# Gram of eight units per call, in four array tiles and two PSUM banks

## The chip, the cores and the metric

The kernel runs on one core of a Trainium2 chip. The core has four compute engines with queues of their own: TensorE (PE, with its weight loads shown apart as PEld), VectorE (DVE), ScalarE (ACT) and GpSimd (POOL); SyncE (SP) issues the DMAs. The metric is device time in microseconds, lower is better. The kernel before takes 352.01 us (median of three runs, 351.21 to 354.52).

## The reference

A gated delta-rule attention (batch 4, 8 heads, 768 tokens, head size 48) feeds a gated convolution with two 384 x 384 projections. All is float32.

```python
for t in range(S):
    kt, vt, bt = (k_n[:, :, t], v[:, :, t], beta[:, :, t, None])
    y[:, :, t] = np.einsum('bhd,bhde->bhe', q[:, :, t], state)
    v_old = np.einsum('bhde,bhd->bhe', state, kt)
    state = state + bt[:, :, :, None] * np.einsum('bhd,bhe->bhde', kt, vt - v_old)
...
for k in range(K):
    gate_pre += conv_w[k][None, None, :] * xp[:, k:k + S, :]
gate = 1.0 / (1.0 + np.exp(-gate_pre))
val = x @ w_val
return (gate * val @ w_out).astype(np.float32)
```

`k_n` is `k` divided by its norm (plus 1e-6); `x` is `y` with the heads side by side, 384 wide; `xp` is `x` with four zero tokens ahead.

## The kernel before

**Chunks and groups.** The 768 tokens are cut into 12 chunks of 64, and two chunks make a group, so there are six groups (`g` 0 to 5). In a chunk each of the 32 (batch, head) pairs has its own small problem. The pairs come two by two: a *unit* is one such double, with one pair in the upper and one in the lower partitions, 16 units a chunk (`NP`) and 32 a group (`NU`). Inside a chunk the recurrence is solved in closed form: it needs the products of all keys of the chunk with each other and with the queries (the Gram), the inverse of a triangular matrix made of them, and the state at the chunk's start.

**Preparing a group (`prep`).** SP loads keys and queries feature by feature into one of three `KQ` buffers, eight units at a time, so four loads make a group. `gram(c, h)` then multiplies K by [K, Q] for four units (`QB`) into one PSUM bank of 128 x 512: one pair's 48 features stand in partitions 64 to 111 and go to PSUM partitions 0 to 63, the other's in 0 to 47 and go to 64 to 127. Each is a matmul of 48 rows, 64 columns of weights and 128 streamed columns, in its own quarter of the array (array tile). Two of the four quarters are used. A call is eight matmuls, which the trace shows as 16 instructions, since each float32 matmul is run in two passes. ACT copies each bank to SBUF (`gevac`, tile `GL`). `diag` (ACT) collects the diagonal blocks in `D1`, and DVE turns them with a large transpose (`trans_in`, `TLP<-D`). Then follows a long chain on DVE, with some large products on POOL: 18 small steps for the norms and coefficients (`coef`), rows and merges that build the inverse, and two transposes out (`trans_out`, tiles `TTR` and `TNA`). With `TTR` PE forms the off-diagonal blocks in two levels (`lev1`, tile `z`; `lev2`, tile `t`).

**The chain of chunks (`chain`).** For each chunk PE multiplies with the state (`e`), DVE adds that to V (`eevac`), PE applies the inverse (`u`) and updates the state (`SPS`), ACT copies both out, PE forms the output `y`, ACT copies it, and SP moves parts of it with six small DMAs (`X<-YS`) to the tile `X`. Some of these matmuls are issued in turns: `eumul` interleaves the 16 matmuls of `e` for one half with the 16 of `u` for the other. `e` uses the same two array tiles as `gram`, `u` the other two, and they write different PSUM banks.

**The gated convolution (`moe`).** For each chunk and each of three feature blocks: two taps of the convolution on PE (`conv`), three on DVE (`tap`), a sigmoid on ACT (`sig`), the projection `val` on PE, and the product on DVE (`gate`). Then two `out` calls on PE, copied by ACT and stored.

**What sets the order.** Every step is entered in a plan (`add`) with its engine and what it reads and writes. `ORDER`, a table of step numbers found beforehand, is the order in which the steps are issued; each engine runs its own in that order. A negative number -n in it stands for n filler matmuls on zeros (`keep_warm`, `SPS<-ZW`), which keep TensorE's clock up and whose result nobody reads. PSUM banks come from two pools of three: pool "w" serves `gram`, `z`, `t`, `val` and `out`, pool "c" the rest of the chain and `conv`. A bank is taken by the step with `take` and given back by the one with `give`; a step that takes waits until a bank has been given back.

The host lays K and Q out for the KQ load: for each chunk an array of 112 rows, the first of a double's features in rows 64 to 111, the second's in 0 to 47, for all 16 units.

Of the kernel before, what the change touches and what calls it, by code (L numbers as in the profile page):

```python
# [16 lines left out]
B, H, S, D = 4, 8, 768, 48  # L17
C = 64
# [74 lines left out]
]  # L93


# [729 lines left out]
```

## Time and profile before

| what | value |
|---|---|
| median of three runs | 352.01 us |
| time of the profiled execution | 352.4 us |
| span of its instructions | 350.7 us |
| granted TensorE clock, mean | 0.946 |

The profile shows this one execution. "Busy" is time in which an engine runs instructions; in a row of a group it is followed by the mean of one instruction, then by the idle time just before such instructions and by what ended that. In a row of the timeline the first number is the start and the second the length in microseconds, a final x32 the number of instructions merged in the row, and a bracket the idle time before it. A row by stage gives the window, its length, then the busy time and instruction count of each engine, the granted clock, the DMA share and GB/s. How the groups follow each other is read from the first `z` matmul of each, the step for which PE needs DVE's `TTR`: 64.4, 108.6, 155.2, 203.9, 246.0 and 298.8 us for groups 0 to 5; PE's last `out` ends at 346.1. Rows of the profile that carry the argument stand in the prediction.

### The profile page before, as it was taken

What the parts mean: (1) busy time and instruction counts of PE and PEld (TensorE: products, weight loads), DVE (VectorE), ACT (ScalarE), POOL (GpSimd) and SP (SyncE); (2) the same over time, 40 slices, a digit from 0 to 9 for tenths busy, and PEclk for the clock granted to TensorE, in tenths of its full rate; (3) what the DMA queues carried; (4) which work ended last, traced back from release to release, by engine and by line L of the source; (5) the groups of instructions that cost most, each with busy time, mean ns of one, the idle gap of its engine ahead of it and who ended that gap; (6) DMA issues with size and microseconds to landing.
All of it is one profiled execution on the core that took longest, in us unless ns stands there. A gap on an engine that the chain in (4) does not pass through costs nothing.

```text
span 350.7 us, 13815 instructions
## 1 busy us (share of the span) xinstructions
PE 318.4 (91%) x5998; PEld 262.1 (75%) x5998; DVE 260.8 (74%) x565; ACT 194.3 (55%) x428; POOL 123.0 (35%) x92
## 2 busy tenths in 40 slices
PE   8769997689299799999799999999988999999994
PEld 5768997689288687878668778777677787687872
DVE  5038999999789876999956999789885689612550
ACT  6643400898149853379764797447973421974221
POOL 6425047034891026512068400545204564000000
PEclk9985899668769999999999999999999999999999
DMA  7999711036274534144574435135253332101122
GB/s 201 249 269 277 190 52 47 7 104 187 67 170 133 151 110 118 32 141 126 140 200 119 136 99 152 50 85 158 56 152 104 80 78 49 38 15 36 36 45 45
DMA packets 20283, 39.47 MB, mean 113 GB/s; under 512 B 8112, under 2 KB 11312, under 8 KB 20224
## 3 DMA queue, kind: packets, MB, share of 16 engines
q1 hardware_dynamic: 20224, 38.60, 41.5%
q8 instruction: 47, 0.77, 0.9%
q14 instruction: 12, 0.10, 0.1%
HBM read 32.69 MB, written 4.72 MB: 107 GB/s over the span
## 4 chain that ended last, share of the span: by engine, by line
PE 62%; DVE 21%; ACT 6%; DMA 5%; issue 3%; POOL 1%; SPq 0%; ACTq 0%; DVEq 0%
PE val L704 14%; PE out L715 12%; PE conv L689 9%; PE gram L351 6%; DMA KQ<-in_kq_dram 5%; PE e L570 5%; PE u L570 3%; PE SPS L570 3%; PE y L638 3%; PE y L640 2%; DVE PR L426 2%; DVE TT__83 L433 2%; PE z L450 2%; PE t L470 2%; ACT D L214 2%
## 5 line engine op out<-in xcount | busy, mean ns | idle before, releaser
L694 DVE SCALAR_TENSOR_TENSOR conv<-X,CW,conv 128x256 f32<-128x256 f32 x108 | 48.5, 486 | 19.7 <-PE conv L689 12.8
L351 PE MATMUL gram<-KQ 48*64 48x128 f32 x768 | 54.0, 295 | 6.1 <-DMA KQ<-in_kq_dram 5.6
L704 PE MATMUL val<-X,WV 128*128 128x256 f32 x216 | 53.4, 388 | 1.3 <-ACT GL L214 1.3
L351 PEld LDWEIGHTS gram<-KQ 48*64 48x64 f32 x768 | 47.7, 147 | 8.5 <-issue 3.5
L715 PE MATMUL out<-WO,GT 128*128 128x384 f32 x144 | 50.3, 490 | 0.0
L704 PEld LDWEIGHTS val<-X,WV 128*128 128x128 f32 x216 | 39.5, 189 | 8.5 <-ACT GL L214 1.4
L214 ACT ACTIVATE GL<-gram 128x512 f32<-128x512 f32 x48 | 28.1, 596 | 23.1 <-PE gram L351 22.7
L689 PE MATMUL conv<-X,DW 128*128 128x256 f32 x144 | 37.9, 399 | 0.5 <-DMA X<-YS 0.5
L715 PEld LDWEIGHTS out<-WO,GT 128*128 128x128 f32 x144 | 26.8, 189 | 15.0 <-issue 0.2
L570 PE MATMUL u<-VT,BD 64*64 64x48 f32 x768 | 31.1, 230 | 7.2 <-DVE VT L622 6.2
L570 PEld LDWEIGHTS u<-VT,BD 64*64 64x64 f32 x768 | 27.3, 144 | 10.7 <-issue 8.7
L548 POOL TENSOR_SCALAR_AFFINE_SELECT AQ<-GL 64x1024 f32<-64x1024 f32 x24 | 28.3, 1180 | 16.5 <-PE y L638 12.2
L214 ACT ACTIVATE D<-GL 32x512 f32<-32x512 f32 (+1 forms) x36 | 22.7, 631 | 19.7 <-DVE TT__83 L433 19.1
L758 PEld LDWEIGHTS SPS<-ZW 128*128 128x128 f32 x242 | 31.3, 210 | 2.8 <-issue 2.7
L758 PE MATMUL SPS<-ZW 128*128 128x128 f32 x242 | 32.9, 298 | 0.0
L708 DVE TENSOR_TENSOR GT<-val,GT 128x256 f32<-128x256 f32 x36 | 15.0, 420 | 20.8 <-PE val L704 18.8
L689 PEld LDWEIGHTS conv<-X,DW 128*128 128x128 f32 x144 | 26.2, 193 | 5.1 <-issue 0.6
L342 POOL TENSOR_TENSOR VT<-VT,NRM 128x768 f32<-128x768 f32 x12 | 17.7, 1477 | 35.1 <-DMA VT<-in_vt_dram 27.7
L638 PE MATMUL y<-AQ,US 112*64 112x64 f32 x384 | 29.1, 233 | 0.0
L638 PEld LDWEIGHTS y<-AQ,US 112*64 112x64 f32 x384 | 25.9, 146 | 3.6 <-issue 2.2
L698 ACT ACTIVATE GT<-conv 128x256 f32<-128x256 f32 x36 | 13.4, 387 | 27.1 <-DVE conv L694 27.0
L640 PE MATMUL y<-AQ,US 128*48 128x64 f32 x384 | 28.0, 230 | 0.0
(97 smaller groups left out, 591.2 us busy)
## 6 DMA issues: line engine op xcount, KB each, us to landing
KQ<-in_kq_dram SPq DMA_DIRECT2D x24, 448.0 KB, 4.7
KF<-in_kf_dram SPq DMA_DIRECT2D x11, 448.0 KB, 3.9
VT<-in_vt_dram SPq DMA_DIRECT2D x12, 384.0 KB, 4.1
AQ<-in_qf_dram SPq DMA_DIRECT2D x24, 192.0 KB, 3.6
KT<-in_kt_dram SPq DMA_DIRECT2D x12, 384.0 KB, 3.5
out_dram<-OS SPq DMA_DIRECT2D x48, 96.0 KB, 2.2
AQ<-in_w_val_dram SPq DMA_DIRECT2D x3, 384.0 KB, 11.0
AQ<-in_w_out_dram SPq DMA_DIRECT2D x3, 384.0 KB, 12.7
```

The source lines that it names most:

```text
L214: A.activation(out=out, in_=in_, func=AF.Copy, **kw)
L342: G.tensor_tensor(out=VT[c], in0=VT[c], in1=NRM[:, c * NP:(c + 1) * NP].unsqueeze(2).to_broadcast([128, NP, D]), op=ALU.mult)
L351: PE.matmul(p[64 * a:64 * a + 64, 128 * j:128 * (j + 1)], x[:, 0:C], x, start=True, stop=True)
L548: G.affine_select(out=AQ[c][r0:r0 + 64, j], in_=GL[r0:r0 + 64, c * NP:(c + 1) * NP, 64:128], pattern=[[0, NP], [1, C]], compare_op=ALU.is_ ...
L570: return lambda: PE.matmul(*a, stop=True, **k)
L638: PE.matmul(p[0:64, C * j:C * j + C], US[ch % 3][0:112, 0, h, D * j:D * j + 64], AQ[c][0:112, 0, pp, :], start=True, stop=True)
L640: PE.matmul(p[64:112, C * j:C * j + C], us[:, 1, h, j, :], AQ[c][:, 1, pp, :], start=True, stop=True)
L689: PE.matmul(p[:, 0:B * C].rearrange("p (b t) -> p b t", t=C), DW[:, m, i, :], x[:, m, :, k:k + C], start=(i == 0), stop=(i == len(PTAPS) - 1))
L694: V.scalar_tensor_tensor(out=p, in0=x[:, m, :, k:k + C], scalar=CW[:, m, k:k + 1], in1=p, op0=ALU.mult, op1=ALU.add)
L704: PE.matmul(p[:, 0:B * C].rearrange("p (b t) -> p b t", t=C), WV[:, k, 128 * m:128 * m + 128], xs[:, k], start=(k == 0), stop=(k == NKT - 1))
L715: PE.matmul(bank["o", ch, i][:, 0:DM], GT[k][:, 2 * i:2 * i + 2, :].rearrange("p b t -> p (b t)"), WO[:, k, :], start=(k == 0), stop=(k == ...
L758: PE.matmul(SPS[0][:, 384:512], ZW, ZW, start=False, stop=True, skip_group_check=True)
```

## The change

A call of `gram` now takes eight units. It holds two banks and runs four matmuls for each step `j`: two units, one in the first four of the load (`s` = 0) and one in the second four (`s` = 1), each with both its pairs. For the second four units the host swaps the rows: the pair that goes to PSUM partitions 0 to 63 has its features in rows 0 to 47, and the other in 64 to 111. So the four matmuls of a step fall into all four quarters of the array; the two that share PSUM partitions come from different rows and write different banks. There are four calls a group instead of eight, each with two `gevac` copies. The first of the two banks is taken by a step of its own, `gram_bank`, without an instruction.

```diff
+        def gram_bank(c, h):
+            bank["g", g, c, 2 * h] = wps("gram")
+
         def gram(c, h):
-            p = bank["g", g, c, h] = wps("gram")
-            kq_ = KQ[(4 * g + 2 * c + h // 2) % 3]
+            bank["g", g, c, 2 * h + 1] = wps("gram")
+            kq_ = KQ[(4 * g + 2 * c + h) % 3]
             for j in range(QB):
-                for a, r in ((0, slice(64, 112)), (1, slice(0, D))):
-                    x = kq_[r, QB * (h % 2) + j, :]
-                    PE.matmul(p[64 * a:64 * a + 64, 128 * j:128 * (j + 1)], x[:, 0:C], x, start=True, stop=True)
+                for a in range(2):
+                    for s in range(2):
+                        r = 64 * (a ^ s ^ 1)
+                        x = kq_[r:r + D, QB * s + j, :]
+                        PE.matmul(bank["g", g, c, 2 * h + s][64 * a:64 * a + 64, 128 * j:128 * (j + 1)], x[:, 0:C], x,
+                                  start=True, stop=True)
...
-        for i in range(8):
-            c, h, n = i // 4, i % 4, 4 * g + i // 2
-            if h % 2 == 0:
-                add("SP", 1.0, load, (KQ[n % 3], kq[2 * g + c, h // 2]), w=[("KQ", n % 3)], kind="LK")
-            add("PE", 0.87, gram, (c, h), cols=1536, r=[("KQ", n % 3)], w=[("gp", g, i)], take="w")
-            add("ACT", 0.5, gevac, (c, h), r=[("gp", g, i)], w=[("GL", gb, i), ("GQ", gb, i)], give="w")
+        for i in range(4):
+            c, h, n = i // 2, i % 2, 4 * g + i
+            tk = [("KQ", n % 3)]
+            add("SP", 1.0, load, (KQ[n % 3], kq[2 * g + c, h]), w=tk, kind="LK")
+            add("PE", 0, gram_bank, (c, h), r=tk, w=["gb"], take="w")
+            add("PE", 1.0, gram, (c, h), cols=3072, r=tk + ["gb"], w=[("gp", g, i)], take="w")
+            for s in range(2):
+                add("ACT", 0.5, gevac, (c, 2 * h + s), r=[("gp", g, i)], give="w",
+                    w=[("GL", gb, 2 * i + s), ("GQ", gb, 2 * i + s)])
...
-    kq = kq.reshape(nch, 112, 2, HB, 2 * C).transpose(0, 2, 1, 3, 4)
+    kq = kq.reshape(nch, 112, 2, HB, 2 * C).transpose(0, 2, 1, 3, 4).copy()
+    kq[:, :, 0:D, QB:], kq[:, :, 64:112, QB:] = kq[:, :, 64:112, QB:].copy(), kq[:, :, 0:D, QB:].copy()
```

The table `ORDER` is new throughout; two of its lines:

```diff
-    1, 4, 8, 2, 16, 110, 5, 160, 3, 65, 162, 6, 70, 9, 10, 7, 11, 12, 13, 161, 0, 14, 75, 15, 17, 24, 64, 18, 19,
+    -1, 8, 16, 65, 160, 9, 70, -1, 3, 1, 2, 7, 75, -1, 10, 11, 12, -1, 13, -2, 14, 17, 0, 4, 6, -1, 15, 24, 64, 18,
```

It holds 147 filler matmuls where the old one held 121; 25 of the new ones stand behind group 1's first `z`, where the old table has none. What it moves is shown at three places. Names are those of the program: a tile's name, its number, then its size.

The first place is SP's queue at the start, before: the DMAs in the order of issue. `KQ0`, `KQ1`, `KQ2` are the three Gram buffers (the fourth load of group 0 is the second one to `KQ0`), `VT` is V, `KF` is K for the chain, `AQ0<-in_qf` is Q, the weights come through `AQ1`.

```order
L219 DMA AQ1_79<-in_w_val_dram 128x768
L219 DMA VT1_75<-in_vt_dram 128x768
L219 DMA KQ0_67<-in_kq_dram 112x1024
L219 DMA AQ0_78<-in_qf_dram 48x1024
L219 DMA KQ1_68<-in_kq_dram 112x1024
L219 DMA BE_108<-in_beta_dram 128x192
L219 DMA AQ0_78<-in_qf_dram 48x1024
L219 DMA KQ2_69<-in_kq_dram 112x1024
L219 DMA AQ1_79<-in_w_val_dram 128x768
L219 DMA KF1_77<-in_kf_dram 112x1024
L219 DMA VT0_74<-in_vt_dram 128x768
L219 DMA KQ0_67<-in_kq_dram 112x1024
```

The same queue now, up to the third block of `w_val`:

```order
L221 DMA AQ1_79<-in_w_val_dram 128x768
L221 DMA KQ0_67<-in_kq_dram 112x1024
L221 DMA KQ1_68<-in_kq_dram 112x1024
L221 DMA BE_108<-in_beta_dram 128x192
L221 DMA KQ2_69<-in_kq_dram 112x1024
L221 DMA AQ1_79<-in_w_val_dram 128x768
L221 DMA KQ0_67<-in_kq_dram 112x1024
L221 DMA KT0_70<-in_kt_dram 128x768
L221 DMA AQ1_79<-in_w_val_dram 128x768
```

Both VT loads, both Q loads and the KF load have gone behind the fourth KQ load.

The second place is PE around the first `z` of group 1, before. `X_98` and `X_99` belong to chunks 0 and 1, `GL_81` to group 1, and the `gram` rows to group 3.

```order
L570 MATMUL e<-US_95,KF_76 64x48 x16
L689 MATMUL conv<-X_98,DW 128x256 x2
L570 MATMUL SPS_121<-US_94,KT_71 48x48 x16
L689 MATMUL conv<-X_98,DW 128x256 x2
L758 MATMUL SPS_120<-ZW 128x128 x6
L450 MATMUL z<-TTR,GL_81 32x32 x16
L351 MATMUL gram<-KQ_67 64x128 x16
L450 MATMUL z<-TTR,GL_81 32x32 x16
L351 MATMUL gram<-KQ_68 64x128 x16
```

The same place now:

```order
L700 MATMUL conv<-X_98,DW 128x256 x6
L581 MATMUL SPS_121<-US_94,KT_71 48x48 x16
L715 MATMUL val<-X_98,WV 128x256 x6
L700 MATMUL conv<-X_99,DW 128x256 x2
L715 MATMUL val<-X_98,WV 128x256 x3
L700 MATMUL conv<-X_99,DW 128x256 x4
L769 MATMUL SPS_120<-ZW 128x128
L726 MATMUL out<-WO,GT_101 128x384 x6
L769 MATMUL SPS_120<-ZW 128x128
L458 MATMUL z<-TTR,GL_81 32x32 x32
L358 MATMUL gram<-KQ_67 64x128 x16
L769 MATMUL SPS_120<-ZW 128x128 x3
```

All of chunk 0's `conv`, `val` and `out` and chunk 1's `conv` now stand ahead of this `z` (three `conv` of two matmuls each, three `val` of three, two `out` of three more than before), and fillers stand behind it.

The third place is DVE ahead of group 1's transpose `TTR`, before. The `conv` rows are the taps, `GT` rows the gates, `VT<-e` is `eevac`.

```order
L433 TENSOR_REDUCE TT__83<-PR_85 128x16x4
L426 TENSOR_TENSOR PR<-ZT,TT__83 128x512
L694 SCALAR_TENSOR_TENSOR conv<-X_98,CW,conv 128x256
L433 TENSOR_REDUCE TT__83<-PR 128x16x4
L694 SCALAR_TENSOR_TENSOR conv<-X_98,CW,conv 128x256
L433 TENSOR_REDUCE TT__83<-D_86 128x16x4
L622 TENSOR_TENSOR VT_74<-e,VT_74 128x384
L440 STREAM_TRANSPOSE TNA<-TT__83 128x32x32
L438 STREAM_TRANSPOSE TTR<-TT__83 128x32x32
```

The same place now:

```order
L705 SCALAR_TENSOR_TENSOR conv<-X_98,CW,conv 128x256 x8
L434 TENSOR_TENSOR PR<-ZT,TT__83 128x512
L719 TENSOR_TENSOR GT_101<-val,GT_101 128x256
L441 TENSOR_REDUCE TT__83<-PR 128x16x4
L705 SCALAR_TENSOR_TENSOR conv<-X_98,CW,conv 128x256
L441 TENSOR_REDUCE TT__83<-D_86 128x16x4
L719 TENSOR_TENSOR GT_101<-val,GT_101 128x256
L448 STREAM_TRANSPOSE TNA<-TT__83 128x32x32
L705 SCALAR_TENSOR_TENSOR conv<-X_99,CW,conv 128x256 x2
L719 TENSOR_TENSOR GT_101<-val,GT_101 128x256
L446 STREAM_TRANSPOSE TTR<-TT__83 128x32x32
```

Eleven taps instead of two and three gates instead of none stand ahead of `TTR`; the taps of `X_99` need chunk 1's output.

122 rows, old and new, of the table ORDER are left out of this document.

## The prediction

> **What bounds the kernel now.** I read the page's busy shares and slices first, then the chain that ended last, then busy time by stage, and last the timeline of single calls.
>
> ```profile
> span 350.7 us, 13815 instructions
> PE 318.4 (91%) x5998; PEld 262.1 (75%) x5998; DVE 260.8 (74%) x565; ACT 194.3 (55%) x428; POOL 123.0 (35%) x92
> ...
> PE   8769997689299799999799999999988999999994
> ...
> DVE  5038999999789876999956999789885689612550
> ...
> PEclk9985899668769999999999999999999999999999
> ```
>
> PE is busy 91% of the span, but not for one reason throughout. In the first third DVE shows the nines; from slice 13 on it is PE, at full clock. I cut the span at the first level-1 matmul (`z`) of group 0 and of group 1, at those of groups 4, 5 and at the end of PE's work.
>
> ```profile
> core 0: us, PE busy (x) PEld busy (x) DVE busy (x) ACT busy (x) POOL busy (x), PEclk, DMA share, GB/s
> 0.00:64.38 64.38, 52.84 (x486) 47.46 (x487) 44.46 (x93) 24.40 (x45) 26.70 (x25) 0.89 0.67 175
> 64.38:108.63 44.25, 36.81 (x892) 33.37 (x892) 39.52 (x73) 30.24 (x64) 25.09 (x17) 0.73 0.41 112
> 108.63:346.20 237.57, 228.73 (x4620) 181.25 (x4620) 176.79 (x401) 139.17 (x321) 71.23 (x50) 1.00 0.36 96
> ...
> 203.90:246.00 42.10, 41.97 (x944) 33.81 (x940) 36.60 (x88) 26.96 (x61) 14.61 (x9) 1.00 0.41 112
> ...
> 298.80:346.20 47.40, 46.76 (x797) 35.58 (x796) 18.23 (x40) 22.84 (x57) 0.22 (x1) 1.00 0.14 31
> ```
>
> So there are three parts. Up to 108.63 the loads and then DVE's preparation of groups 0 and 1 decide; much of PE's work there is filler on zeros. From 108.63 on PE is busy 228.73 of 237.57 us, with 8.8 idle. The last 47.4 us are nearly pure PE.
>
> **The cheaper Gram.** A call before is eight logical matmuls, in two array tiles.
>
> ```profile
> L351 PE MATMUL gram<-KQ 48*64 48x128 f32 x768 | 54.0, 295 | 6.1 <-DMA KQ<-in_kq_dram 5.6
> ...
> 109.02 1.96 PE L351 MATMUL gram<-KQ 48*64 48x128 f32 x32
> 110.91 0.45 PE L450 MATMUL z<-TTR,GL 32*32 32x32 f32 x32
> ...
> 123.22 0.22 PE L570 MATMUL e<-US,KF 48*64 48x48 f32 x2
> 123.23 0.23 PE L570 MATMUL u<-VT,BD 64*64 64x48 f32 x2
> 123.28 0.23 PE L570 MATMUL e<-US,KF 48*64 48x48 f32 x2
> 123.29 0.23 PE L570 MATMUL u<-VT,BD 64*64 64x48 f32 x2
> ...
> 130.83 1.10 PE L570 MATMUL e<-US,KF 48*64 48x48 f32 x32
> ```
>
> Two calls (32 instructions, two passes for each logical matmul) hold PE from 109.02 to 110.91, so 0.945 us each, or 118 ns for each round of two tiles. Do four tiles fit in a round? The kernel already has that pattern: `e` and `u` together start four matmuls (two `e`, two `u`, in four array tiles and two banks) every 0.06 us, while `e` alone needs 1.10 us for 32 instructions, 0.069 for two. Four cost no more than two. The Gram streams 128 columns where these stream 48, so the nearest row is its own round; I take 0.945 us for the new call of eight units. The other end is 1.89, no overlap. With 24 new calls for 48 old, PE loses 24 x 0.945 = 22.7 us of work. Of this only the calls of groups 3 to 5 lie behind 108.63: 12 x 0.945 = 11.3 us on the path. The other half lies in stretches where PE waits or fills, and I cost it at nothing.
>
> One thing speaks against this price: two of the four tiles share the same rows of the array. If a tile's weight load could not hide behind the other tile's matmul, each of the eight rounds would add about an `e`/`u` round, and a call would take 0.945 + 8 x 0.06 = 1.43 us; the saving on the path would be 12 x (1.89 - 1.43) = 5.5 us instead of 11.3. `e` and `u` share rows in the same way and still start a round every 0.06 us, so I leave it to the rivals. By the Trainium skill (TensorE: Matmul & The Clock Gate, Part 3, "What overlaps and what doesn't") a weight load overlaps running matmuls only if its row group differs, which is that case; the `e` and `u` rows don't agree with it, though at 48 columns only.
>
> **Work moved ahead of group 1's `z`.** Three `conv`, three `val` and two `out` calls of chunks 0 and 1 now stand before group 1's first `z`, and nine more taps and three more gates before DVE's transpose TTR of group 1.
>
> ```profile
> L694 DVE SCALAR_TENSOR_TENSOR conv<-X,CW,conv 128x256 f32<-128x256 f32 x108 | 48.5, 486 | 19.7 <-PE conv L689 12.8
> L704 PE MATMUL val<-X,WV 128*128 128x256 f32 x216 | 53.4, 388 | 1.3 <-ACT GL L214 1.3
> L715 PE MATMUL out<-WO,GT 128*128 128x384 f32 x144 | 50.3, 490 | 0.0
> L689 PE MATMUL conv<-X,DW 128*128 128x256 f32 x144 | 37.9, 399 | 0.5 <-DMA X<-YS 0.5
> L708 DVE TENSOR_TENSOR GT<-val,GT 128x256 f32<-128x256 f32 x36 | 15.0, 420 | 20.8 <-PE val L704 18.8
> ...
> 42.98 16.57 PE L758 MATMUL SPS<-ZW 128*128 128x128 f32 x146
> ```
>
> Calls are 36 `conv` of 37.9/36 = 1.05 us, 36 `val` of 1.48, 24 `out` of 2.10. So 3 x 1.05 + 3 x 1.48 + 2 x 2.10 = 11.8 us of PE work leaves the PE-bound part for a part in which PE fills. What hides it there is DVE's preparation; if that cover were short, at most the 11.8 us would come back. On SP a VT load now stands among the six X<-YS transfers of chunk 0 and waits for chunk 1's `u`; chunk 0's `conv` stands behind that `u` on PE anyway, so I cost it at nothing, and at one load's landing (4.1 us, below) if it is late. DVE pays 9 x 48.5/108 + 3 x 0.417 = 5.3 us ahead of TTR. In its stage DVE idles 44.25 - 39.52 = 4.7 us, some of it behind POOL products that these taps can cover. The price is between 0.6 and 5.3; I take 3.
>
> Against that the new order puts 25 filler matmuls behind group 1's `z` (none before): 73 of them took 16.57 us, so 25 x 0.227 = 5.7 us, if none stands in a wait. They have no reader. PE work behind `z` of group 1: 228.73 - 11.3 - 11.8 + 5.7 = 211.3 us.
>
> **The start.** These are the chain's first links, and the loads that stand ahead of the fourth KQ load.
>
> ```profile
> 2.20 6.75 DMA KQ<-in_kq_dram
> 8.99 1.99 PE gram L351 x32
> 10.99 10.72 DMA KQ<-in_kq_dram
> 21.85 1.10 PE gram L351 x16
> 23.47 0.54 ACT AQ L271
> 24.01 0.59 ACT GL L214
> ...
> 26.58 2.09 DVE TLP L364
> ...
> KQ<-in_kq_dram SPq DMA_DIRECT2D x24, 448.0 KB, 4.7
> KF<-in_kf_dram SPq DMA_DIRECT2D x11, 448.0 KB, 3.9
> VT<-in_vt_dram SPq DMA_DIRECT2D x12, 384.0 KB, 4.1
> AQ<-in_qf_dram SPq DMA_DIRECT2D x24, 192.0 KB, 3.6
> AQ<-in_w_val_dram SPq DMA_DIRECT2D x3, 384.0 KB, 11.0
> ...
> 32.58 2.91 POOL L342 TENSOR_TENSOR VT<-VT,NRM 128x768 f32<-128x768 f32 x2 [3.28 <-DVE QUOT L334]
> ```
>
> The fourth KQ load took 10.72 us because 3.8 MB had been issued ahead of it; with its own 0.45 MB, 4.26 MB had landed by 21.85 us, 0.195 MB per us. Two VT, two qf and the KF load now come behind it: 2 x 384 + 2 x 192 + 448 KB = 1.6 MB, so it could land 8 us sooner. But ACT evacuates this Gram only after it has converted the third `w_val` block, whose load now has about 3.4 MB up to its end: 3.4/0.195 = 17.5 us. From 23.47, where ACT began that block, to DVE's transpose at 26.58 are 3.1 us; with 0.5 for the landing and a second evacuation the transpose starts near 21.5. I take 5 us of gain; the ends are 0 (a load put back is missed) and 8. DVE's order from there to TTR of group 0 is nearly the old one, so the gain carries through.
>
> **The sum**, on the profiled execution, 350.7 us of span and 352.4 of time (352.01 is the median of the runs, 0.4 lower). First `z` of group 1: 108.6 - 5 + 3 = 106.6. From there to the first `z` of group 5, PE was busy 228.7 - 46.8 = 182.0 of 190.2 us, idle 8.2; its work is now 182.0 - 11.3 - 11.8 + 5.7 - 1 = 163.6 (1 us more falls in the tail, one `out` for one `conv`), and with the old idle time 172. DVE has a say here: it was busy 176.8 - 18.2 = 158.6, now 153.3, and in the stage where it had least slack, 203.90 to 246.00, it still idled 5.5 us. Four such stages make 153.3 + 22 = 175.3. The two engines bound this part at nearly the same length, so waits of one on the other add; I take 177 where 190.2 stood. Tail 48.4, then 4.5 us from the last matmul to the end. Span 106.6 + 177 + 48.4 + 4.5 = 336.5; time 336.5 + 1.7 = 338.2, less 0.4: **338 us**, 4% faster.
>
> **The rivals.**
>
> - *The start does not come earlier, or DVE eats it.* Against it: of the loads put back, VT was first read at 32.58, by a POOL step that waited for DVE. For it: DVE's 5.3 us may count in full. The time is 338 + 5 without the start, 338 + 7.3 with both: 343 to 345.
> - *Four tiles do not run side by side.* No row shows 128 columns in four tiles. With unhidden weight loads 12 x 0.48 = 5.8 us come back, 344; with nothing overlapping 11.3, 349. The `e` and `u` rows speak against both.
> - *DVE alone becomes the bound, and PE's saving stays unused.* Were the four stages to keep their length, 190.2 instead of 177, the time would be 351. Against it: DVE's longest idle rows there are waits for PE, 18.8 us for `val`, 12.8 for `conv`.
> - *Slower: two banks at once.* `gram`, `z`, `t`, `val` and `out` share three banks, and a Gram call now holds two until ACT, in its own order, has copied both; `val` and `out` then follow each other on the third.
>
> ```profile
> L214 ACT ACTIVATE GL<-gram 128x512 f32<-128x512 f32 x48 | 28.1, 596 | 23.1 <-PE gram L351 22.7
> ...
> 121.52 1.56 PE L704 MATMUL val<-X,WV 128*128 128x256 f32 x6 [1.33 <-ACT GL L214]
> ```
>
>   Even now a `val` waited 1.33 us for such a copy. If each of the 12 late Gram calls and of the 33 `val` calls behind `z` paid a wait of half that, 45 x 0.67 = 30 us would go against the 14 gained: 368. It decides once about 21 of the 45 calls wait so long. For it: two copies of 0.596 us take longer than a call of 0.945, so Gram calls back to back are bound by ACT. Against it: the order spreads the calls between `z`, `e` and `u`, which need other banks or only one. The Trainium skill (TensorEngine Tiling (Array Packing), "PSUM Bottleneck") has the general form: tiling speeds up TensorE but not the evacuation of PSUM, which may then be the bound.
>
> **How the numbers follow.** The likeliest, 332 to 342, has 0.52. The start or DVE rival has 0.18, four tiles 0.07, DVE alone 0.10, banks 0.08 (as far as they make it slower than before). An even better end, all of the start's 8 us and the fillers in waits (338 - 3 - 5.7 = 329), has 0.05. The 80% range is 329 to 348. About 1%, 3.5 us, is what a measurement of this kernel can tell from no change: faster than that 0.81, within it 0.11, slower 0.08.
>
> **What would show it.** Gram rows of the new kernel: four starts each round and about 0.95 us for 32 instructions (right), or 1.4 to 1.9 (wrong). DVE's first large transpose near 21.5 us instead of 26.58; the first `z` of group 1 near 106.6. PE's idle rows behind it: waits for ACT's Gram copies of more than 10 us in all would mean banks, waits for TTR or for gates of more than 15 us would mean DVE. PE's busy time should fall to about 300 us. I am wrong if the start is still at 26 us or if `val` waits for ACT.

## The result, and the profile after

The changed kernel takes 337.19 us (median of 4 runs, 335.16 to 340.48), beside 351.61 us for the kernel before on the same chip (4 runs, 349.62 to 354.52). The ratio is 0.956 with a 95% interval of 0.946 to 0.967: 4.4% faster. The forecast was 338.0 us. Three further measurements of the same kernel, below, gave 334.9 to 335.6 us. Some executions are in a slower state, which the ratios leave out (of e6 two of six are left, so its 352.80 us and its ratio below don't match), and no stage length is read from the profiles of e1, e4, e6 and e11, which were taken in it.

The page of the changed kernel, its span, busy times and slices:

```profile
span 336.5 us, 13878 instructions
...
PE 308.9 (92%) x6050; PEld 251.0 (75%) x6050; DVE 261.8 (78%) x565; ACT 193.3 (57%) x428; POOL 124.7 (37%) x92
...
PE   8936999699779979999999999999999999999994
...
DVE  5368999999698994999997899896998779511640
...
PEclk9987599755997998999999999999999999999999
```

PE is busy 308.9 us where it was 318.4 (the forecast said about 300), DVE has the same work as before. The slices tell the same story as before: DVE's nines in the first third, PE's nines from there on.

Cut at the first `z` of group 0 and of group 1 (first three rows, columns as in the prediction's rows by stage), and one stage of the PE-bound part, groups 3 to 4:

```profile
0.00:58.50 58.50, 48.15 (x499) 42.57 (x499) 44.51 (x93) 23.35 (x45) 26.07 (x25) 0.85 0.71 186
58.50:109.95 51.45, 44.12 (x924) 37.94 (x924) 45.61 (x87) 34.83 (x72) 25.09 (x18) 0.77 0.32 88
109.95:336.50 226.55, 216.67 (x4629) 170.52 (x4628) 171.68 (x388) 135.10 (x313) 73.50 (x49) 0.99 0.41 106
...
191.57:241.41 49.84, 49.30 (x1022) 39.18 (x1018) 43.12 (x99) 32.83 (x75) 21.67 (x16) 1.00 0.41 109
```

The first part is 5.9 us shorter, the second 7.2 longer, the third 15.5 shorter (226.55 us, where before 350.7 - 108.63 = 242.1 stood). By the first `z` of each group, with two of the later measurements of the same kernel beside it:

| stretch, us | before | forecast | after | e0 | e8 |
|---|---|---|---|---|---|
| start to `z` of group 0 | 64.4 | 59.4 | 58.5 | 58.3 | 57.3 |
| `z` of group 0 to group 1 | 44.3 | 47.2 | 51.5 | 49.4 | 49.7 |
| `z` of group 1 to group 5 | 190.2 | 177 | 173.8 | 172.5 | 172.3 |
| `z` of group 5 to the end | 51.9 | 52.9 | 52.8 | 52.9 | 53.0 |
| span | 350.7 | 336.5 | 336.5 | 333.1 | 332.3 |

The groups that answer to those shown of before, and the fillers:

```profile
L705 DVE SCALAR_TENSOR_TENSOR conv<-X,CW,conv 128x256 f32<-128x256 f32 x108 | 49.9, 484 | 14.2 <-PE conv L700 12.1
L715 PE MATMUL val<-X,WV 128*128 128x256 f32 x216 | 52.5, 390 | 0.0
...
L358 PE MATMUL gram<-KQ 48*64 48x128 f32 x768 | 33.4, 311 | 10.2 <-DMA KQ<-in_kq_dram 8.5
...
L769 PE MATMUL SPS<-ZW 128*128 128x128 f32 x294 | 43.7, 302 | 0.4 <-ACT US L643 0.4
```

The same 768 `gram` instructions now fill 33.4 us of PE instead of 54.0, though the mean of one is no shorter (311 ns, before 295): they overlap. `val` no longer waits at all. The fillers fill 43.7 us in 294 instructions, two for each filler; before it was 32.9 us in 242. One call in the timeline:

```profile
156.17 0.94 PE L769 MATMUL SPS<-ZW 128*128 128x128 f32 x6
157.03 1.10 PE L358 MATMUL gram<-KQ 48*64 48x128 f32 x32
158.07 1.13 PE L700 MATMUL conv<-X,DW 128*128 128x256 f32 x4
```

Eight units, 32 instructions, hold PE from 157.03 to 158.07, 1.04 us. The forecast had 0.945; before, 32 instructions took 1.89. The row above it shows three fillers (six instructions) in 0.86 us, 0.287 each where the forecast had 0.227.

The start, in the chain of work that ended last:

```profile
8.67 1.08 PE gram L358 x32
9.77 0.88 ACT GL L216 x2
10.65 7.23 DMA AQ<-in_w_val_dram
17.98 0.55 ACT AQ L273
18.53 0.98 ACT GL L216 x2
...
21.49 2.06 DVE TLP L372
```

The fourth KQ load has left the chain. The third block of `w_val` stands in it instead, and DVE's first large transpose starts at 21.49 instead of 26.58.

What PE waited for between the first `z` of group 1 and that of group 5:

```profile
PE y L649 <- issue: 1.9, 1, 1.9
PE y L649 <- DMA AQ<-in_qf_dram: 0.7, 1, 0.7
PE SPS L769 <- ACT US L643: 0.4, 2, 0.2
PE SPS L581 <- issue: 0.4, 1, 0.4
PE gram L358 <- ACT GL L216: 0.2, 1, 0.2
```

Here the columns are the sum in microseconds, the number of waits and the longest. For a Gram copy PE waited 0.2 us in all. "issue" is a wait for nothing that the profile shows; the last section has more on it.

### The profile page after: what moved, and what is told of

Read it like the earlier page. It is cut to its first block, busy times and chain, and to the rows that moved or that the text cites. A ratio compares the mean times of both kernels' runs of the same rounds, so it can differ in the third digit from the quotient of the medians.

```text
span 336.5 us, 13878 instructions
## 1 busy us (share of the span) xinstructions
PE 308.9 (92%) x6050; PEld 251.0 (75%) x6050; DVE 261.8 (78%) x565; ACT 193.3 (57%) x428; POOL 124.7 (37%) x92
## 4 chain that ended last, share of the span: by engine, by line
PE 60%; DVE 14%; ACT 8%; DMA 7%; POOL 4%; issue 3%; SPq 3%; POOLq 0%; ACTq 0%; DVEq 0%
PE out L726 14%; PE val L715 11%; PE conv L700 7%; PE gram L358 4%; PE e L581 4%; PE u L581 3%; PE SPS L769 3%; PE y L649 3%; SPq L221 3%; PE SPS L581 2%; PE y L651 2%; PE z L458 2%; DMA AQ<-in_w_val_dram 2%; PE t L478 2%; DMA X<-YS 2%
## 5 line engine op out<-in xcount | busy, mean ns | idle before, releaser
L705 DVE SCALAR_TENSOR_TENSOR conv<-X,CW,conv 128x256 f32<-128x256 f32 x108 | 49.9, 484 | 14.2 <-PE conv L700 12.1
L421 POOL TENSOR_TENSOR PR<-TLP,TT__83 128x768 f32<-128x768 f32 x5 | 10.6, 2118 | 97.0 <-DVE TT__83 L416 97.0
L769 PE MATMUL SPS<-ZW 128*128 128x128 f32 x294 | 43.7, 302 | 0.4 <-ACT US L643 0.4
L769 PEld LDWEIGHTS SPS<-ZW 128*128 128x128 f32 x294 | 39.4, 210 | 5.1 <-issue 3.6
L358 PE MATMUL gram<-KQ 48*64 48x128 f32 x768 | 33.4, 311 | 10.2 <-DMA KQ<-in_kq_dram 8.5
L216 ACT ACTIVATE GL<-gram 128x512 f32<-128x512 f32 x48 | 27.1, 596 | 16.7 <-PE gram L358 16.2
L358 PEld LDWEIGHTS gram<-KQ 48*64 48x64 f32 x768 | 26.1, 156 | 13.6 <-issue 9.3
L649 PE MATMUL y<-AQ,US 112*64 112x64 f32 x384 | 31.0, 237 | 4.7 <-issue 4.0
L651 PE MATMUL y<-AQ,US 128*48 128x64 f32 x384 | 29.1, 233 | 0.0
L633 DVE TENSOR_TENSOR VT<-e,VT 128x384 f32<-128x384 f32 x22 | 12.3, 557 | 20.1 <-PE e L581 14.1
L637 ACT ACTIVATE US<-u 64x384 f32<-64x384 f32 x24 | 11.6, 483 | 27.9 <-PE u L581 27.8
```

Source lines behind the costliest of these rows:

```text
L216: A.activation(out=out, in_=in_, func=AF.Copy, **kw)
L358: PE.matmul(bank["g", g, c, 2 * h + s][64 * a:64 * a + 64, 128 * j:128 * (j + 1)], x[:, 0:C], x, start=True, stop=True)
L633: V.tensor_tensor(out=v, in0=bank["e", ch, h][:, 0:HB * D].rearrange("p (u x) -> p u x", x=D), in1=v, op=ALU.add)
L649: PE.matmul(p[0:64, C * j:C * j + C], US[ch % 3][0:112, 0, h, D * j:D * j + 64], AQ[c][0:112, 0, pp, :], start=True, stop=True)
L651: PE.matmul(p[64:112, C * j:C * j + C], us[:, 1, h, j, :], AQ[c][:, 1, pp, :], start=True, stop=True)
L705: V.scalar_tensor_tensor(out=p, in0=x[:, m, :, k:k + C], scalar=CW[:, m, k:k + 1], in1=p, op0=ALU.mult, op1=ALU.add)
```

## The experiments

All were timed in five rounds against the kernel before. They ran in three groups (e0 to e3, e4 to e7, e8 to e11); the kernels of a group shared a chip and its runs of the kernel before, so each is compared with the unedited kernel of its own group (e0, e4, e8). Those three differ by up to 0.007 among themselves, so smaller differences than about 1% are not read.

| run | edit | us | ratio to before, 95% |
|---|---|---|---|
| e0 | none | 334.90 | 0.944 [0.939, 0.949] |
| e1 | Gram in two array tiles | 349.16 | 0.981 [0.975, 0.987] |
| e2 | five loads back ahead of the fourth KQ load | 343.09 | 0.966 [0.960, 0.972] |
| e3 | without 25 fillers | 339.36 | 0.957 [0.952, 0.962] |
| e4 | none | 335.60 | 0.949 [0.943, 0.956] |
| e5 | new Gram call, old order | 379.84 | 1.077 [1.071, 1.083] |
| e6 | moved work put back | 352.80 | 0.988 [0.978, 0.998] |
| e7 | halo copy first on POOL | 337.90 | 0.954 [0.947, 0.961] |
| e8 | none | 335.07 | 0.950 [0.945, 0.956] |
| e9 | e5 with 104 fillers more | 381.38 | 1.083 [1.078, 1.088] |
| e10 | e6 with 40 fillers more | 349.67 | 0.994 [0.990, 0.998] |
| e11 | 22 fillers more in group 0's stage | 342.54 | 0.970 [0.963, 0.976] |

**The yardsticks.**

> The changed kernel itself, unedited, as the yardstick for the three kernels run beside it. Both theories: 335 to 339 us, a ratio of 0.956 to the kernel before.

> The changed kernel unedited once more, as the yardstick for the three beside it: a ratio of 0.944 to 0.957 to the kernel before.

> The changed kernel once more, unedited, as the yardstick of the three runs beside it: 0.944 to 0.949 of the kernel before, as in its two earlier runs.

The unedited kernel came out at 0.944, 0.949 and 0.950. Together with the first measurement (0.956) this is one kernel at 335 to 337 us.

**e1: is it the four array tiles?** The call keeps eight units and two banks, but the second four units use the same rows as the first, as the old call did. So only two of the four tiles are in use.

```diff
-                for a in range(2):
-                    for s in range(2):
-                        r = 64 * (a ^ s ^ 1)
+                for s in range(2):
+                    for a in range(2):
+                        r = 64 * (a ^ 1)
...
-    kq[:, :, 0:D, QB:], kq[:, :, 64:112, QB:] = kq[:, :, 64:112, QB:].copy(), kq[:, :, 0:D, QB:].copy()
```

> The changed kernel with its order, banks and calls, but the second four units lie in the old rows, so each call of eight units runs in two array tiles. Theory (the cheaper call is on the path): a call takes about 1.9 us instead of 1.04; the 12 calls behind group 1's first z give back 12 x 0.9 = 10 to 11 us, so 346 to 349 us. Rival (the redrawn order alone makes the gain, the call's price is hidden in PE's waits): within 2 us of the unedited kernel.

A call of e1 in the timeline, and what follows it:

```profile
200.09 1.96 PE L358 MATMUL gram<-KQ 48*64 48x128 f32 x32
201.99 2.00 PE L700 MATMUL conv<-X,DW 128*128 128x256 f32 x8
```

The call holds PE for 1.90 us instead of 1.04. Twelve such calls behind group 1's `z` make 12 x 0.86 = 10.3 us; the time rose by 0.981/0.944, 3.9% or 13 us. So the gain of the cheap call is on the path, some 10 of the 13 us by the call's own length.

**e2: is it the start?** The two VT loads, the two Q loads and the KF load go back ahead of the fourth KQ load; pieces of the table:

```diff
-    -1, 8, 16, 65, 160, 9, 70
+    -1, 8, 16, 110, 65, 160, 162, 9, 70
...
-    7, 75
+    7, 161, 75
...
-    24, 64
+    24, 215, 107, 64
```

> The changed kernel, but the two VT, two qf and the KF loads stand where they stood before, ahead of the fourth KQ load. Theory (the load order sets the first transpose, and the gain of 5 us is carried through): DVE's first large transpose at 26 to 27 us instead of 21.5, and the time 4 to 6 us longer. Rival (a later wait takes the start's gain in): the transpose is late but the time is within 2 us of the unedited kernel.

The first large transpose of e2:

```profile
26.89 2.10 DVE L370 STREAM_TRANSPOSE TLP<-D 128x1024 f32<-128x1024 f32 x1 [1.11 <-ACT D L214]
```

It is at 26.89 again, 5.4 us later than in the changed kernel's profile; the first `z` of group 0 follows at 63.7, that of group 1 at 113.5, and the span ends at 339.5 instead of 333.1. The time rose by 2.3%, 7.8 us. The start's gain goes through to the end in full.

**e3: what do the 25 fillers cost?** They are left out of the table behind group 1's first `z`.

```diff
-    497, 679, 681, 680, 498, -1, 499, -1, 500, -1, 683, 501
+    497, 679, 681, 680, 498, 499, 500, 683, 501
...
```

> The changed kernel without the 25 filler matmuls behind group 1's first z. Theory of the prediction (they stand on PE's path at 0.227 us each): 5 us faster, 331 to 333 us. Rival (they stand in waits of PE for ACT or DVE, which stay): within 1.5 us of the unedited kernel, with PE's idle time up by 4 to 6 us.

It became slower than e0, not faster: 1.4%, 4.7 us, and all six of its runs (338.3 to 342.1) lie above the median of e0. Against the first measurement of the changed kernel, 0.956, its ratio of 0.957 is no different, so the loss shows within its own group only. In the trace the work that went did not shorten the part that it went from: from the first `z` of group 1 to that of group 3 e3 took 81.25 us, e0 79.96. The largest single loss is at 188 us. The stretches around it in e3 by windows:

```profile
188.00:190.00 2.00, 0.53 (x61) 0.42 (x49) 1.51 (x2) 1.00 (x2) 1.92 (x2) 1.00 0.97 297
190.00:195.00 5.00, 4.65 (x41) 3.80 (x42) 1.89 (x4) 4.21 (x9) 0.43 (x1) 0.52 0.62 134
195.00:200.00 5.00, 5.00 (x138) 3.63 (x137) 4.61 (x20) 2.92 (x7) 0.00 (x0) 0.80 0.61 157
```

and the row that ends the gap:

```profile
190.35 0.31 PE L455 MATMUL z<-TTR,GL 32*32 32x32 f32 x3 [1.82 <-issue]
```

PE stood for 1.82 us for nothing that the profile shows, and the granted clock fell to 0.52 for the next five microseconds and 0.80 for the five after that. Both are mixtures: in the trace the clock is one half from 190.2 to 197.0 us and full around it. From the first `z` of group 3 to that of group 4 e3 took 53.6 us where e0 took 50.2.

From the first `z` of group 1 to that of group 5 e3 took 178.2 us, e0 172.5. PE was busy 168.1 us there, hardly less than e0's 168.8 although 25 fillers were gone, and idle 10.1 instead of 3.7: its waits on "issue" came to 5.9 us instead of 1.5, those for ACT to 1.9 instead of 0.2. So the rival was near with the idle time and wrong with the total. The gap at 188 us itself is no wait that a filler had stood in: by the trace PE's next instructions arrived late there (last section). How much of the loss is due to the fillers is therefore not told apart.

**e5: what does the new call do in the old order?** The new Gram code, with the old table: each call stands where the first of its two old calls stood, or later if no two banks would be free by then. The 25 late fillers, the early KQ load and the moved work are all absent. A piece of the two tables, where 678 and 680 were Gram calls of group 3 and 679 a copy; now 678 takes the first bank, 679 is the call and 680 a copy:

```diff
-    494, -6, 344, 678, 348, 347, 680, 201, 679
+    494, -6, 344, 678, 679, 680, 348, 347, 201
...
```

> The new Gram call in the order of the kernel before: each call of eight units stands where the first of the two old calls stood (later only where a bank is missing), everything else where it was, with no filler behind group 1's first z. Theory (the call's price is on the path in either order): 8 to 11 us faster than before, a ratio of 0.969 to 0.977. Rival (only an order drawn for it can use the saving; without one, waits for banks, DVE and the clock take it): a ratio above 0.985.

It is 7.7% slower than the kernel before: both expectations missed, and by far. Its timeline behind the first `z` of group 1:

```profile
110.54 0.45 PE L454 MATMUL z<-TTR,GL 32*32 32x32 f32 x32 [0.55 <-DVE TTR L442]
110.92 1.10 PE L354 MATMUL gram<-KQ 48*64 48x128 f32 x32
111.96 0.45 PE L454 MATMUL z<-TTR,GL 32*32 32x32 f32 x32
112.79 0.43 PE L354 MATMUL gram<-KQ 48*64 48x128 f32 x2 [0.38 <-ACT GL L212]
114.63 1.98 PE L354 MATMUL gram<-KQ 48*64 48x128 f32 x30 [1.41 <-ACT GL L212]
117.55 0.31 PE L474 MATMUL t<-ZS,TNA 32*32 32x32 f32 x2 [0.94 <-ACT ZS L212]
```

A call starts its first matmul and then stops in the middle for its second bank, which ACT has yet to copy. Between the first `z` of group 1 and that of group 5 the largest of PE's waits are these:

```profile
PE gram L354 <- ACT GL L212: 4.1, 6, 1.4
PE z L454 <- ACT BD L212: 3.4, 2, 1.7
PE gram L354 <- ACT ZS L212: 3.3, 4, 0.9
PE t L474 <- ACT GL L212: 2.7, 4, 0.7
PE t L474 <- ACT ZS L212: 1.7, 3, 0.9
```

With two smaller ones (0.9 and 0.8) that is 16.9 us of waiting for ACT's copies, against 2.4 in the kernel before (1.3, 0.8 and 0.3) and 0.6 in the changed one. By stage, from the first `z` of group 1 on:

```profile
110.54:164.98 54.44, 48.60 (x896) 38.03 (x896) 39.81 (x97) 28.71 (x64) 13.98 (x10) 0.81 0.34 99
164.98:223.09 58.11, 51.83 (x1064) 40.77 (x1060) 38.10 (x80) 35.29 (x78) 20.83 (x15) 0.79 0.44 116
223.09:274.91 51.82, 46.78 (x944) 36.27 (x940) 37.23 (x88) 26.82 (x61) 14.74 (x9) 0.80 0.34 91
```

The clock, 1.00 in these stages before, is 0.79 to 0.81. If the missing share counts on all of the busy time, it costs 48.60 x 0.19 + 51.83 x 0.21 + 46.78 x 0.20 = 29.5 us. From the first `z` of group 1 to that of group 5 e5 takes 216.1 us, where 190.2 less the cheaper call's 11.3 would be 178.9: 37 us too many. PE's busy time has 26 of them (197.1 us, where 182.0 less 11.3 would be 170.7) and its idle time 11 (19.0 where 8.2 was): the waits for copies grew by 14.5, those on "issue" fell by 4. The work is the same, so the 26 us go with the lower clock, near the 29.5 of the estimate. This is the forecast's rival of the banks, and it is real. The Trainium skill (TensorEngine Tiling (Array Packing), "PSUM Bottleneck") says that tiling speeds up TensorE and not the evacuation of PSUM; e5 agrees, with its 16.9 us of waits for copies.

**e9: is it the waits or the clock?** e5 with fillers in the waits: four ahead of each Gram call of groups 2 to 5, two ahead of each second-level step (`t`) of groups 1 to 5. They compute nothing that is read.

```diff
-    -6, 344, 678, 679, 680, 348
+    -6, 344, 678, -4, 679, 680, 348
...
```

> The new call in the old order as before (which took 1.077 of the kernel before), with 104 fillers more: four ahead of every Gram call of groups 2 to 5 and two ahead of every second-level step of groups 1 to 5, where TensorE had stood idle for banks and for copies (about 6.9 us a group in the stage behind group 1's first z). Nothing else is moved and no wait is taken away. Theory of the clock (the bank waits cost little by themselves, the low granted clock behind them costs most): the stages behind group 1's z, at 0.79 to 0.81 of full clock before, come near 1.00 and shorten by some 8 to 10 us each, so the time falls by 25 to 40 us, to 0.96 to 1.00 of the kernel before. Theory of the banks (ScalarE's copies bound the Gram, the clock is a side effect): the fillers stand in line with the waits, the time falls by less than 5 us or rises, and stays above 1.06.

The same stages in e9:

```profile
110.11:165.98 55.87, 54.09 (x944) 43.88 (x945) 40.01 (x97) 28.81 (x64) 14.66 (x10) 0.88 0.34 96
165.98:220.49 54.51, 51.51 (x1112) 41.21 (x1108) 38.12 (x80) 35.23 (x78) 20.77 (x15) 0.97 0.45 124
220.49:271.98 51.49, 47.76 (x992) 38.45 (x988) 36.82 (x88) 26.86 (x61) 14.60 (x9) 0.97 0.34 92
```

The clock came back (0.88, 0.97, 0.97) and the waits for ACT fell to 7.8 us, but the time did not fall: 1.083 against 1.077, and 216.1 us from the first `z` of group 1 to that of group 5 as in e5. Of the fillers 80 lie there; where four of them stand together at full clock they hold PE for 1.09 us in this trace, so they cost at least 80 x 0.27 = 21.6 us, which is what clock and waits gave back. The theory of the clock falls as it was put: the clock can be bought back, but for its full price. Nor is ACT's copying as such the bound: the changed kernel makes the same copies, and PE waits 0.2 us for Gram copies in this part. It is their place in the order.

**e6: was the moved work hidden?** The block of chunks 0 and 1 (three `val`, three `conv` and two `out` calls with their copies, eight taps, three gates, two sigmoids) goes back behind the second level of group 1; the rest of the new order stays. Of the nine taps that the change puts ahead of TTR seven stay there.

```diff
-    493, 206, 342, 211, 348, 212, 207, -1, 344
+    493, 342, 348, -1, 344
...
-    510, 350, 357
+    510, 350, 191, 192, 198, 245, 199, 205, 238, 252, 246, 239, 206, 211, 212, 207, 208, 247, 240, 248, 241, 253, 249, 254, 242, 357
```

> The changed kernel, but three val, three gates, two out, three conv and seven of the taps of chunks 0 and 1 go back behind group 1's first level-2 step. Theory of the prediction (this work leaves the PE-bound part for one where PE only fills): PE gets back 11.8 us behind z while z comes 3 to 5 us sooner, so 6 to 9 us slower than unedited. Rival (PE is bound from about 90 us on, ahead of z, so the work is only moved within the bound part): z comes 8 us sooner or more, and the time is within 3 us of unedited.

PE then stands in front of group 1's first `z`:

```profile
105.41 0.81 PE L456 MATMUL z<-TTR,GL 32*32 32x32 f32 x44 [9.33 <-DVE TTR L444]
```

and the time rises by 0.988/0.949, 4.1% or 14 us, twice what was expected. The hole of 9.33 us is the cover that the moved work had; `z` then starts 0.06 us after the end of DVE's TTR.

**e10: how much of that is the clock?** e6 with 40 fillers in the hole.

```diff
-    493, 342, 348, -1, 344
+    493, 342, 348, -41, 344
```

> The moved work put back behind group 1's second level (0.988 of the kernel before, with TensorE idle for 9.3 us ahead of group 1's first z and a clock of 0.81 in the 56.6 us behind it), with 40 fillers ahead of that z, 9.1 us by 0.227 us each, to cover the idle stretch. If half of the loss came from the clock, the stage behind z shortens to 49 to 51 us, which is the 37 to 39 of the changed kernel with the 11.8 us of moved work, and the time falls by 5 to 8 us to 0.965 to 0.975. If the loss is the moved work itself and its order, the time stays within 2 us, 0.982 to 0.994.

The two stages around group 1's first `z` in e10:

```profile
56.57:105.39 48.82, 45.11 (x963) 41.05 (x963) 42.32 (x80) 34.26 (x70) 24.35 (x18) 0.69 0.34 93
105.39:157.11 51.72, 47.10 (x994) 37.72 (x993) 36.52 (x83) 26.57 (x62) 16.94 (x10) 0.93 0.41 108
```

The ratio, 0.994, is within e6's interval: the second expectation holds, and the loss is the moved work and its place. Against e8 the stage behind `z` is 51.72 - 35.47 = 16.2 us longer, and the stage ahead of it only 49.74 - 48.82 = 0.9 us shorter. So the 11.8 us of PE work, with three gates and the taps that were moved, cost little where the change put it: 0.9 us, or 2.5 if the 1.6 us are added by which the fillers of e10 keep `z` behind TTR. Behind `z` PE is busy 13.3 us more than in e8, at a clock of 0.93 instead of 1.00, and idle 3.0 more.

**e7: the wait for the halo.** In the changed kernel PE and DVE lose time ahead of group 1's TTR. Two rows of its timeline show it, and three show what follows, up to `z`:

```profile
99.86 1.13 PE L700 MATMUL conv<-X,DW 128*128 128x256 f32 x4 [2.29 <-POOL X L695]
...
104.88 0.49 DVE L705 SCALAR_TENSOR_TENSOR conv<-X,CW,conv 128x256 f32<-128x256 f32 x1 [1.57 <-PE conv L700]
...
105.61 2.04 DVE L446 STREAM_TRANSPOSE TTR<-TT__83 128x1024 f32<-128x1024 f32 x1
...
105.77 4.04 PE L726 MATMUL out<-WO,GT 128*128 128x384 f32 x12
...
109.95 0.75 PE L458 MATMUL z<-TTR,GL 32*32 32x32 f32 x64
```

POOL copies the last four tokens of chunk 0 (the halo, step 185) behind a large masking step (367). e7 exchanges the two.

```diff
-    190, 313, 335, 367, 237, 185, 195
+    190, 313, 335, 185, 367, 237, 195
```

> The changed kernel, but on POOL the halo copy of chunk 0 goes ahead of the mask of group 1 (att) and of chunk 1's halo; PE's conv of chunk 1 waits 2.3 us for that copy. Theory (PE bounds from about 90 us on): 1.5 to 2.3 us faster than unedited. Rival (DVE's TTR sets the end of that part): no difference above 0.7 us.

No difference beyond the scatter of the yardsticks: 0.954 beside 0.949. The wait is gone in e7's trace, and the stage from group 0's first `z` to group 1's takes 48.5 us where e0 has 49.4 and e8 49.7. So the wait makes about 1 us of it, which the time doesn't show. Nor does DVE's TTR set the end of that stage, as the rival had it: in the rows above TTR ends at 107.65, and `z` starts 2.3 us later, because PE is still on chunk 0's `out` calls. In e0 and e8 `z` is 2.2 us behind TTR, in e7 1.1; in the kernel before it was 0.06.

**e11: a version that might be better.** In the changed kernel the clock is low in group 0's stage (0.77 in the row of 58.50:109.95 above). e11 adds ten fillers ahead of group 0's first `z`, six ahead of its second level and six ahead of a step of its chain.

```diff
-    141, -50, 142
+    141, -60, 142
...
-    475, 146, 147
+    475, 146, -6, 147
...
-    331, 222
+    331, -6, 222
```

> The changed kernel with 22 fillers more in the stage of group 0 (ten ahead of its first z, six ahead of its second level, six ahead of a step of its chain), where the clock stood at 0.50 to 0.71 between 58 and 75 us. Theory of the clock: that stretch comes near 1.00 and group 1's first z stands 1 to 3 us earlier, so the kernel is 0.003 to 0.009 of the kernel before faster than the yardstick beside it. Theory of VectorE (its busy time fills that stage, 45.5 of 49.4 us, so TensorE's speed there is worth nothing): within 0.003 of the yardstick, or slower where fillers stand ahead of work.

It is 2.0% slower than e8. The clock of that stage rose to 0.87 and the time did not fall: the first expectation is out, and the second holds, DVE being busy for 43 to 46 us of that stage (48 to 51 us long) in every order tried with the moved work in it. PE's gaps of kind "issue" are larger in it, too (below), so not all of the loss need come from the fillers. No run beat the changed kernel.

## Why the prediction was right

The time (338.0 forecast; 337.2, then 334.9 to 335.6 measured) and most terms held. That the span came out at 336.5 to the digit is luck: in the first profile the start is 0.9 us and the PE-bound part 3.2 us shorter than forecast, the part ahead of group 1's `z` 4.2 longer, and that cancels. Step by step:

- **The start, -5 us.** Right in size and in reason: the transpose at 21.49 (forecast 21.5), and e2, which puts the loads back, loses at least those 5 us (7.8 in the time). The bound named, ACT's conversion of the third `w_val` block, is the chain's next link in the profile.
- **Ahead of group 1's TTR, +3 us.** Right for TTR, too small for the stage: 5.2 and 5.5 us in e0 and e8, 7.2 in the profiled run, where its bounds were 0.6 to 5.3. TTR itself ends 47.2 and 47.5 us behind group 0's first `z` in e0 and e8, where it was 44.2: 3.0 and 3.3 later, as forecast (5.0 in the profiled run). The other 2.2 us are PE's: when TTR ends, PE is still on moved work, and the forecast had no term for that. The wait for the halo is about half of them (e7). What TTR's 3 us consist of isn't settled: in e10, with seven of the nine taps still ahead of it, TTR ends at 47.2 too, and in e5, with the old order and the new call, at 45.6.
- **The cheaper Gram, -11.3 us.** Right. A call takes 1.04 us, 0.1 more than forecast, and e1 shows 10.3 us of call time and 13 us of kernel time. The rival that four tiles with shared rows don't run side by side is out. The rule of the Trainium skill weighed there (TensorE: Matmul & The Clock Gate, Part 3), for which the forecast's estimate was 1.43 us a call, doesn't hold here: with 1.04 us, weight loads of tiles in the same rows do hide, with 128 streamed columns too.
- **The moved work, -11.8 us.** Right in size, and hidden for the most part, by DVE's preparation of group 1: the hole in e6 is 9.33 us, and 2.2 us stand behind TTR's end, together nearly the 11.8. The forecast had said that at most 11.8 us would come back if the cover failed; e6 and e10 lost 14 to 15, in e10 with more idle time and a lower clock beside the work itself.
- **The fillers, +5.7 us "if none stands in a wait".** Too small, and not to be won back. The 0.227 us came from a block of 73; PE's rows give 0.287 us a filler where three stand together, and by the starts of the instructions behind them the 25 hold PE for 8.4 us. In the whole span the fillers' row grew by 10.8 us, the main reason why PE is busy 308.9 us and not about 300. Yet without the 25 the kernel was 4.7 us slower than e0, not 5.7 faster: in e3's profile PE's idle time and a lower clock took their place, in part behind late instructions, so what the fillers are worth stays open.
- **From `z` of group 1 to that of group 5, 177 us.** 173.8, and 172.3 to 172.5 in the later profiles: the PE bound of 172 alone. The added 5 us for PE and DVE waiting on each other was not needed; this is why the forecast was some 3 us above the later runs. The bound agrees as a sum and less in its parts: in e0 PE is busy 168.8 us there (forecast 163.6) and idle 3.7 (8.2). That the two cancel is luck. Of the 5.2 us of more work, dearer fillers explain 3.0 (8.7 us in e0, where 5.7 was forecast) and dearer calls 1.2; the rest isn't traced.
- **The banks, 0.08.** The mechanism is real, as e5 shows: put into the old order the call loses 44 us against the changed kernel. What the forecast said against it, that the order spreads the calls, is what decides: with the new order ACT's Gram copies cost PE 0.2 us in that part. The forecast priced only waits, and not the lower clock that goes with them, which in e5 is the larger part by PE's busy time.

Singly undone, the parts cost 13 (e1), 8 (e2), 5 (e3) and 14 us (e6), 40 in all, where the whole change gained 14 to 21. They don't add: each is measured in an order that was drawn for all of them, and what is undone brings waits and clock losses of its own.

## What to carry to other kernels

A cheaper matmul call that holds more PSUM banks is to be priced together with the order around it: here the kernel with the same call is 4 to 6% faster than before in an order that spreads the evacuations, and 8% slower in the old one. Work that is moved under another engine's stage is best checked at the hole that it fills; here the 9.33 us hole in e6 was the proof of the cover, and the 2.2 us from TTR to `z` showed what stuck out of it. Fillers are no reserve that can be struck from the sum: taking 25 away won nothing, and adding 22, 40 or 104 won none either.

## What the runs showed of the hardware

- **The clock can fall after a short gap.** In e3 one gap of 1.82 us went with a clock of one half from 190.2 to 197.0 us; in e5, gaps of 0.4 to 1.7 us, one after another, went with 0.79 to 0.81 over stages of 52 to 58 us. Not every such gap does it: in the kernel before one of 1.85 us at 262 us left the clock at 1.00. The Trainium skill (TensorE: Matmul & The Clock Gate, "HAM oscillation") speaks of gaps of more than about 3.4 us; in these traces some shorter ones did it.
- **PE's longer gaps for nothing that the profile shows are late instructions.** Over the whole span PE's waits on "issue" sum to 1.5 us in e0, 2.9 in e8, 4.4 in the first profile and 6.4 in e4, all of the same kernel; to 7.3 us in e3 and 9.9 in e11. The traces also hold the packets of the queues that bring instructions: one queue has 47 to 49 packets of 16 KB in each run, for 11,996 to 12,412 matmuls and weight loads, so one for about every 256. In the 14 traces 28 of these gaps are longer than 0.8 us. Each ends 1.2 to 2.0 us after such a packet has landed (in e3 it landed at 188.71, and PE went on at 190.35), and 25 of the 28 end at the same place in a block, 193 or 194 instructions of PE's queue beyond a multiple of 256. The Trainium skill (Runtime: NRT & Kernel Launch, "Instruction fetch mechanics") says that an engine's instructions are streamed in by DMA, mostly hidden. The traces agree: at most six of the 47 to 49 packets of a run go with such a gap. Why a packet comes late is not shown. The gap in e3 fell where the DMA engines were busy 97% of the time, but no run tested that, and so it stays open how much of e3's and e11's loss is due to the fillers themselves.
- **Single effects of a few microseconds need their own yardstick.** The same kernel stood at 0.944, 0.949, 0.950 and 0.956 of the kernel before.
